# Attention and a token/channel mixer on one core: v of a head in one transfer, a weight group in two, and a new order of all work

## The chip, the cores and the metric

The kernel runs on one core of a Trainium2 chip. The number that counts is the time of one execution on the device, in microseconds. The kernel before was run three times: median 972.38 us, from 970.54 to 972.43. One further execution was profiled; it took 971.08 us, and the span from its first to its last instruction is 969.3 us.

Engines are named as the profile names them: PE is the matrix engine, PEld its weight loads, DVE the vector engine, ACT the scalar engine, POOL the GpSimd engine. SP issues the transfers; in the profile its own queue is SPq.

## The reference

Eight batches, eight heads, 576 positions, 64 numbers per head. Everything is float32.

```python
scores = scale * np.matmul(q, k.transpose(0, 1, 3, 2))
cum = np.cumsum(np.log(np.clip(f, 0.0001, 1.0)), axis=-1)
decay = cum[:, :, :, None] - cum[:, :, None, :]
scores = np.where(causal, -1000000000.0, scores + decay)
attn = np.exp(scores - np.max(scores, axis=-1, keepdims=True))
attn = attn / (np.sum(attn, axis=-1, keepdims=True) + 1e-09)
out = np.matmul(attn, v)                       # 8 x 8 x 576 x 64
# the heads side by side are x: 8 x 576 x 512
h = np.maximum(x.transpose(0, 2, 1) @ w_tok1, 0.0) @ w_tok2    # over the positions, 256 wide
u = x + h.transpose(0, 2, 1)
result = u + np.maximum(u @ w_ch1, 0.0) @ w_ch2                # over the channels, 1536 wide
```

The weights arrive as 64-bit numbers and are turned into 32-bit ones on the chip.

## The kernel before

The program has two stages. In the first (0 to about 434 us of the span) the 64 heads are worked off as 32 pairs, two heads of a batch at a time, one on each half of the 128 partitions. Per pair, q and k come in one transfer (line 716, buffer raw, three of them). v comes in four transfers, two per head (line 720, buffer vr, two of them): five blocks of 64 positions to one place, four blocks to another. The decay comes as a broadcast row (line 728, buffer cb, two of them). PE makes the scores (lines 743 and 749), DVE adds the decay and takes the smallest negated score (line 784), ACT takes the exponential and its sums (line 788). PE turns the probabilities (line 862), ACT or DVE copies them out of PSUM into pf (lines 872 and 870), and PE multiplies them with v (lines 891 and 894). The sums are inverted on DVE, turned on PE (line 834), stored to memory in rows of 3 KB (line 840, recd<-rs) and loaded back as broadcast rows (line 845, rb). POOL multiplies them into the result, xt (line 920). After every second pair half a batch is mixed over the positions: PE turns it (line 1244), and two products follow (line 1227, weights t1 and t2, the value held as a high and a low part in xn and ring). The sum goes to memory (line 1313, ud).

Beside this, 24 groups of channel weights are decoded in the first stage: each comes in four transfers of 128 x 128 numbers (line 557, d_raw<-in_w_ch), passes ACT, DVE and POOL, and is stored in two transfers (line 638, wd<-sg).

In the second stage PE does the channel products, 2520 matmuls over 128 x 128 weights (lines 1045 to 1047 and 1110 to 1112), with weights loaded back by line 960. A few of them stand already in the first stage.

The order is fixed by hand, as it were: the table ORDER names for every engine the sequence of its operations, and each engine works its list strictly in that sequence, waiting where something is not there yet. For SP this means that a transfer whose buffer is not free yet holds up all transfers behind it. A planner (class Plan) replays the lists with assumed durations; from this come only the assignment of buffers to slots and the order of the code. All transfers but two are issued by SP and run on one queue.

Of the kernel before, what the change touches and what calls it, by code (L numbers as in the profile page):

```python
# [9 lines left out]
F32 = mybir.dt.float32  # L10
# [5 lines left out]
P = 128  # L16

PRM = dict(
    FILL=36, ND=1, n_raw=3, n_vr=2, n_cb=2, n_rb=2, n_pr=2, n_pf=4, n_xn=1,
# [47 lines left out]
    ),  # L67
    DVE=(
# [205 lines left out]
class Plan:  # L274
# [48 lines left out]
    def run(self, slots):  # L323
# [45 lines left out]
        while left:  # L369
            more = True  # L370
            while more:
                more = False
                for e, q in queue.items():
# [28 lines left out]
                    if e == "SP":  # L402
                        dma_at = max(end + 650, dma_at) + o.lat
                        done = dma_at + 980
# [34 lines left out]
def build(nc, env, dims):  # L439
# [39 lines left out]
    def at(b):  # L479
        return env[b.kind][b.slot]  # L480
# [1035 lines left out]
```

## Time and profile before

| | |
|---|---|
| median of three runs | 972.38 us (970.54 to 972.43) |
| the profiled execution, its span | 971.08 us, 969.3 us |
| mean granted clock of PE over the span | 0.986 |
| PE busy | 932.6 us, 96% |
| DVE busy | 722.2 us, 75% |
| ACT busy | 528.9 us, 55% |
| POOL busy | 237.2 us, 24% |
| mean rate of all transfers | 251 GB/s |
| the chain that ended last | PE 72%, DMA 13%, DVE 8%, ACT 2%, SPq 2% |

How to read it: the table averages over two stages with different limits. ACT and POOL have most of their work in the first stage alone, so their low shares say little. The chain is the sequence of work that ended last, followed back from the end; a share of it by DMA is time in which the last thing still missing was a transfer under way.

### The profile page before, as it was taken

How to read it: one execution, taken by the hardware profiler on the slowest of the kernel's cores; microseconds unless marked ns; L12 is line 12 of the kernel's file. 1: busy time of each engine (PE TensorE's matmuls, PEld its weight loads, DVE VectorE, ACT ScalarE, POOL GpSimd, SP SyncE). 2: the span in 40 equal slices, each digit the busy share in tenths (PEclk: the TensorE clock that was granted, in tenths of full speed). 3: DMA queues.
4: the chain of work that ended last, by engine and by line, in shares of the span. 5: the costliest groups of instructions: out<-in, count | busy, mean ns of one | idle time of the engine just before them, and what ended most of it. 6: DMA issues, size and time to landing. Idle time of an engine off the chain costs nothing.

```text
span 969.3 us, 27342 instructions
## 1 busy us (share of the span) xinstructions
PE 932.6 (96%) x10368; PEld 807.1 (83%) x10368; DVE 722.2 (75%) x1930; ACT 528.9 (55%) x1372; POOL 237.2 (24%) x320
## 2 busy tenths in 40 slices
PE   8899999999999999999999999999999999999998
PEld 5677777777778888888888888888888899989997
DVE  6998887878778876745599638973699538964586
ACT  5877888978878887842255114521254215521242
POOL 3567767765665641110000000000000000000000
PEclk9899999999999999999999999999999999999999
DMA  7889989898899978457877797888878787877874
GB/s 225 248 241 287 292 249 280 246 303 247 249 292 271 283 233 275 146 174 236 292 240 254 247 283 250 250 274 288 260 234 250 246 270 241 247 230 259 285 224 144
DMA packets 152211, 243.43 MB, mean 251 GB/s; under 512 B 22096, under 2 KB 82768, under 8 KB 152080
## 3 DMA queue, kind: packets, MB, share of 16 engines
q1 hardware_dynamic: 151984, 241.54, 80.6%
q8 instruction: 82, 1.34, 0.6%
q14 instruction: 49, 0.40, 0.1%
q10 hardware_dynamic: 96, 0.15, 0.0%
HBM read 200.38 MB, written 41.24 MB: 249 GB/s over the span
## 4 chain that ended last, share of the span: by engine, by line
PE 72%; DMA 13%; DVE 8%; ACT 2%; SPq 2%; issue 2%; POOL 1%; POOLq 0%; DVEq 0%; ACTq 0%
PE bank L1110 9%; PE bank L1112 9%; PE bank L1111 9%; PE bank L1045 9%; PE bank L1047 9%; PE bank L1046 9%; PE bank L1227 6%; PE bank L743 5%; DVE pr L784 3%; PE bank L891 3%; DMA cb<-decd 3%; DMA vr<-in_v 2%; PE bank L862 2%; DMA rb<-recd 2%; DMA raw<-in_qk 1%
## 5 line engine op out<-in xcount | busy, mean ns | idle before, releaser
L788 ACT ACTIVATE pr<-pr,nmin 128x448 f32<-128x448 f32 (+4 forms) x320 | 177.0, 558 | 27.7 <-DVE nmin L784 27.1
L487 ACT ACTIVATE st<-H 128x464 fp32r<-128x464 f32 (+1 forms) x210 | 119.9, 587 | 122.3 <-PE bank L1111 68.0
L1110 PE MATMUL bank<-st,wq 128*128 128x464 f32 (+1 forms) x420 | 156.0, 371 | 0.0
L1111 PE MATMUL bank<-st,wq 128*128 128x464 f32 (+1 forms) x420 | 155.9, 371 | 0.0
L1112 PE MATMUL bank<-st,wq 128*128 128x464 f32 (+1 forms) x420 | 155.8, 371 | 0.1
L784 DVE CUSTOM_DVE_ANT_0 pr<-bank,cb 128x448 f32<-128x448 f32 (+3 forms) x310 | 129.5, 452 | 24.4 <-DMA cb<-decd 9.7
L743 PE MATMUL bank<-raw 64*64 64x448 f32 (+6 forms) x1408 | 120.1, 408 | 9.6 <-DVE nmin L784 5.0
L496 DVE TENSOR_TENSOR st<-H,st 128x464 fp32r<-128x464 f32 (+1 forms) x150 | 91.7, 630 | 19.4 <-ACT st L487 15.9
L891 PE MATMUL bank<-pf,vr 64*64 64x128 f32 (+3 forms) x2048 | 98.8, 320 | 4.5 <-DMA vr<-in_v 3.0
L981 DVE TENSOR_TENSOR tmp<-bank,tmp 128x464 f32<-128x464 f32 (+1 forms) x80 | 50.1, 631 | 58.1 <-PE bank L1047 52.3
L872 ACT ACTIVATE pf<-bank 128x512 f32<-128x512 f32 x152 | 85.0, 594 | 12.4 <-PE bank L862 7.3
L891 PEld LDWEIGHTS bank<-pf,vr 64*64 64x64 f32 x2048 | 76.1, 136 | 17.3 <-ACT pf L872 4.2
L1112 PEld LDWEIGHTS bank<-st,wq 128*128 128x128 f32 x420 | 78.8, 188 | 9.7 <-DVE st L496 0.5
L743 PEld LDWEIGHTS bank<-raw 64*64 64x64 f32 x1408 | 57.0, 137 | 35.6 <-issue 12.5
L1110 PEld LDWEIGHTS bank<-st,wq 128*128 128x128 f32 x420 | 78.8, 188 | 9.2 <-DVE tmp L981 0.2
L1111 PEld LDWEIGHTS bank<-st,wq 128*128 128x128 f32 x420 | 78.8, 188 | 8.9
L862 PE MATMUL bank<-ident,pr 64*128 64x64 f32 x1536 | 68.9, 230 | 6.3 <-DVE nmin L784 4.0
L1057 ACT ACTIVATE tmp<-bank 128x464 f32<-128x464 f32 (+1 forms) x30 | 16.6, 554 | 105.7 <-PE bank L1047 105.6
L862 PEld LDWEIGHTS bank<-ident,pr 64*128 64x128 f32 x1536 | 62.4, 143 | 11.8 <-DVE nmin L784 3.8
L920 POOL TENSOR_TENSOR xt<-xt,rb 128x512 f32<-128x512 f32 (+1 forms) x64 | 51.4, 819 | 79.9 <-DMA rb<-recd 36.6
L1227 PE MATMUL bank<-t2h,ring 64*128 64x288 f32 x512 | 62.8, 308 | 0.3 <-DVE nmin L784 0.2
L788 ACT ACTIVATION_READ_ACCUMULATOR pr<-pr,nmin 128x1 f32 (+1 forms) x320 | 62.4, 195 | 0.0
(172 smaller groups left out, 2099.7 us busy)
## 6 DMA issues: line engine op xcount, KB each, us to landing
wq<-wd SPq DMA_DIRECT2D x420, 256.0 KB
raw<-in_qk SPq DMA_DIRECT2D x32, 576.0 KB
cb<-decd SPq DMA_DIRECT2D x31, 576.0 KB
d_raw<-in_w_ch SPq DMA_DIRECT2D x96, 128.0 KB
wd<-sg SPq DMA_DIRECT2D x24, 512.0 KB
rb<-recd SPq DMA_DIRECT2D x64, 144.0 KB
wd<-sg SPq DMA_DIRECT2D x24, 384.0 KB
ud<-xt SPq DMA_DIRECT2D x16, 576.0 KB
```

The lines of the kernel that those rows point to most:

```text
L487: nc.scalar.activation(out, in_, func, scale=scale)
L496: nc.vector.tensor_tensor(out, in_, asf(hi), op=ALU.subtract)
L743: nc.tensor.matmul(at(buf)[HALF[h], of : of + n], q[:, i0 : i0 + D], k[:, j0 : j0 + n], start=t not in (0, 1), stop=not nd, skip_group_che ...
L784: nc.vector.tensor_tensor_reduce(o, x, y, -1.0 / D**0.5, c0[:m, NS + z : NS + z + 1] if t == 5 else 3e38, op0=ALU.add, op1=ALU.min, accum_ ...
L788: nc.scalar.activation(x, x, AF.Exp, bias=E["nmin"][sm][:m, t : t + 1], scale=-1.0, accum_out=E["sums"][sm // 2][:m, sm % 2 * (NS + 1) + ( ...
L862: nc.tensor.transpose(at(ps[s])[:, k * D : (k + 1) * D], at(pr)[r, x, :, :].rearrange("p a b -> p (a b)"), E["ident"][r, r])
L891: nc.tensor.matmul(at(av[z])[o, 256 - w : 256], at(vr)[r, vblk(j), :], at(pt)[r, c : c + w], start=j == 4, stop=gi == 2, skip_group_check= ...
L1045: nc.tensor.matmul(o, wt[:, 0, :], h_, start=(first and k == 0), stop=False, skip_group_check=True)
L1110: nc.tensor.matmul(o, wt[:, 0, :], h_, start=(first and x == 0), stop=False, skip_group_check=True)
L1111: nc.tensor.matmul(o, wt[:, 1, :], h_, start=False, stop=False, skip_group_check=True)
L1112: nc.tensor.matmul(o, wt[:, 0, :], l_, start=False, stop=(x == FX - 1), skip_group_check=True)
L1227: last[s] = nc.tensor.matmul(at(ps[s ^ z])[:, : width[0]], a, m, start=(z == 0 and i == 0), stop=(z == 1 and i == len(todo[s]) - 1), skip_ ...
```

## The change

v of a head comes in one transfer that fills ten blocks (one block is loaded twice, so that both halves have the same length), and a weight group comes in two transfers. The buffer vr becomes one block longer. The planner assumes 1950 ns in place of 980 ns from the data to the signal of a transfer, and the special rates of two kinds of transfer are dropped. The table ORDER is another one for all five engines. What is computed is the same; on PE both programs hold the same number of matmuls of every line. All line numbers of the first stage move down by four to six.

```diff
-    FILL=36, ND=1, n_raw=3, n_vr=2, n_cb=2, n_rb=2, n_pr=2, n_pf=4, n_xn=1,
+    FILL=36, ND=(0,), n_raw=3, n_vr=2, n_cb=2, n_rb=2, n_pr=2, n_pf=4, n_xn=1,
...
 ORDER = dict(
     PE=(
-        "14:27 147 41:4 148 137 157:2 138 45 141 46 199 142 216 202 47:3 207 175 178 181 169 184:3 282 290 285 233 236 "
+        "14:29 145 139 135:2 140 155 146 156 43:4 195 47:3 203 198 212 173 176 167 179 182:3 276 279 284 293 229 223 "
...
                     if e == "SP":
                         dma_at = max(end + 650, dma_at) + o.lat
-                        done = dma_at + 980
+                        done = dma_at + 1950
...
         def ld(rows, cols, src):
-            o = at(rb)[rows, cols, :]
+            o = at(rb)[rows, cols, :] if hi else at(rb).rearrange("p (a b) two -> p a b two", b=P)[:, cols]
             nc.sync.dma_start(o, src.bitcast(U32).rearrange("... (n two) -> ... n two", two=2))
...
         for x, (b, z0, z1) in enumerate(((pb, 0, 3), (sb, 3, 7))):
             dma(
-                lambda b=b, z0=z0, z1=z1: nc.sync.dma_start(E["w_d"][which][q][:, z0:z1, k], asf(at(b)[:, : z1 - z0])), P * 1024 * (z1 - z0), rate=340,
+                lambda b=b, z0=z0, z1=z1: nc.sync.dma_start(E["w_d"][which][q][:, z0:z1, k], asf(at(b)[:, : z1 - z0])), P * 1024 * (z1 - z0),
...
-            def src(row, half):
+            def src(half):
                 if which == 1:
-                    return w_ch1[sl((k + 2 * half) * P, P), sl((a + row) * P, P)]
-                return w_ch2[sl((a + half) * P, P), sl((2 * row + k) * P, P)]
-
-            loads = [(full, sl(n * P, P), src(row, half)) for n, (row, half) in enumerate(((0, 0), (0, 1), (1, 1), (1, 0)))]
+                    return w_ch1[sl((k + 2 * half) * P, P), sl(a * P, 2 * P)].rearrange("p (r c) -> p r c", c=P)
+                return w_ch2[sl((a + half) * P, P), :].rearrange("p (r k c) -> p r k c", k=2, c=P)[:, :, k, :]
+
+            loads = [(full, cols, half) for half, cols in enumerate((slice(0, 4, 3), slice(1, 3)))]
+            loads = [(full, cols, src(half)) for _, cols, half in loads]
             return lambda: unit(loads, which, q, k, i)
...
         for s in (0, 1):
-            for x, (r, a, z) in enumerate(((HALF[0], 0, NS), (HALF[1], NS, 2 * NS - 1))):
-                dma(
-                    lambda vr=vr, n2=n2, s=s, r=r, a=a, z=z: nc.sync.dma_start(at(vr)[HALF[s], a:z, :], E["v"][n2][r, s * NS + NS - (z - a) : s * NS + NS, :]),
-                    D * (z - a) * D * 4, dur=515, rate=220, wr=[(vr, s, x)], bufs=[vr],
-                )
-        v_in = [(vr, s, x) for s in (0, 1) for x in (0, 1)]
+            dma(
+                lambda vr=vr, n2=n2, s=s: nc.sync.dma_start(
+                    at(vr)[HALF[s]].rearrange("p (x n) e -> p x n e", x=2), E["v"][n2].rearrange("(x d) n e -> d x n e", x=2)[:, :, s * NS : (s + 1) * NS, :]
+                ),
+                D * 2 * NS * D * 4, dur=515, wr=[(vr, s)], bufs=[vr],
+            )
+        v_in = [(vr, s) for s in (0, 1)]
...
-        ("vr", [P, 2 * NS - 1, D], F32),
+        ("vr", [P, 2 * NS, D], F32),
```

On SP, the transfers from the first to the last piece of v of the fourth pair (vr_194 is one of the two v buffers, d_raw the weights still to be decoded, rs the turned inverse sums) stood like this before:

```order
L720 DMA vr_194<-in_v 64x256
L557 DMA d_raw_161<-in_w_ch 128x256
L720 DMA vr_194<-in_v 64x320
L557 DMA d_raw_161<-in_w_ch 128x256
L840 DMA recd<-rs_102 12x64
L557 DMA d_raw_161<-in_w_ch 128x256 x2
L840 DMA recd<-rs_102 12x64
L716 DMA raw_190<-in_qk 128x1152
L720 DMA vr_194<-in_v 64x320
L720 DMA vr_194<-in_v 64x256
```

After the change the same stretch of SP, again from the first to the last piece of v of the fourth pair, reads:

```order
L714 DMA vr_194<-in_v 64x2x320
L551 DMA d_raw_162<-in_w_ch 128x2x256
L836 DMA recd<-rs_102 12x64 x2
L551 DMA d_raw_161<-in_w_ch 128x512
L714 DMA vr_194<-in_v 64x2x320
```

Four pieces of v over eleven transfers have become two over six. Counted for all 32 pairs in the two lists, the last piece stood on average 12.2 transfers behind the first, and stands 5.7 behind it now.

On PE, the turning of the inverse sums of the ninth pair (line 834, from rec) stood in the midst of a mixing product (line 1227, ring is the hidden value, t2 the weight) before:

```order
L1227 MATMUL bank_69<-t2l,ring_157 128x288
L1227 MATMUL bank_68<-t2h,ring_158 128x288
L1227 MATMUL bank_69<-t2h,ring_158 128x288
L834 MATMUL bank_63<-ident,rec_96 64x64 x2
L1227 MATMUL bank_69<-t2h,ring_157 128x288
L1227 MATMUL bank_68<-t2h,ring_157 128x288
L1227 MATMUL bank_69<-t2l,ring_157 128x288
L1227 MATMUL bank_68<-t2l,ring_157 128x288
```

In the changed list the same turning of the ninth pair (now line 830) has the product with v ahead of it (line 887) and scores behind it (line 739):

```order
L887 MATMUL bank_63<-pf_203,vr_193 64x256 x2
L887 MATMUL bank_65<-pf_203,vr_193 64x256 x2
L887 MATMUL bank_63<-pf_203,vr_193 64x256 x2
L887 MATMUL bank_65<-pf_203,vr_193 64x256 x2
L830 MATMUL bank_67<-ident,rec_96 64x64 x2
L739 MATMUL bank_68<-raw_191 64x320
L739 MATMUL bank_69<-raw_191 64x320
L739 MATMUL bank_68<-raw_191 64x256
```

The scores, the product with v and the turning of the sums use PE in quarters of 64 x 64, the turning of the probabilities and the mixing in halves of 64 x 128, the channel products as a whole. Up to the last mixing matmul the list changed between these forms 128 times before, and changes 108 times now.

## Rows read from the trace of the kernel before

**Rows 1.** Busy time by stretch: length, each engine's busy us, PE clock, DMA share, GB/s.

```profile
0.00:120.00 120.00, 107.44 (x1874) 84.54 (x1878) 102.19 (x371) 90.26 (x269) 73.95 (x107) 0.93 0.85 260
120.00:360.00 240.00, 225.68 (x4632) 190.07 (x4628) 194.39 (x720) 201.32 (x610) 150.54 (x198) 0.98 0.88 265
360.00:440.00 80.00, 75.87 (x1385) 65.55 (x1375) 53.04 (x177) 54.37 (x157) 12.68 (x17) 1.00 0.63 200
440.00:970.00 530.00, 523.59 (x2493) 466.91 (x2493) 372.59 (x665) 183.00 (x339) 0.00 (x0) 1.00 0.80 251
```

**Rows 2.** Waits of PE, whole span: who waited for whom, us, times, longest.

```profile
PE bank L743 <- DVE nmin L784: 5.0, 7, 1.7
PE bank L862 <- DVE nmin L784: 4.0, 4, 1.5
PE bank L1244 <- POOL xt L920: 3.3, 3, 1.5
PE bank L891 <- DMA vr<-in_v: 3.0, 3, 1.3
...
PE bank L743 <- DMA raw<-in_qk: 2.0, 1, 2.0
```

**Rows 3.** Groups by line: busy us, mean ns, then idle time ahead and its releasers.

```profile
L784 DVE CUSTOM_DVE_ANT_0 pr<-bank,cb 128x448 f32<-128x448 f32 (+3 forms) x310 | 129.5, 452 | 24.4 <-DMA cb<-decd 9.7 <-PE bank L743 5.9 <-PE bank L749 5.8
...
L920 POOL TENSOR_TENSOR xt<-xt,rb 128x512 f32<-128x512 f32 (+1 forms) x64 | 51.4, 819 | 79.9 <-DMA rb<-recd 36.6 <-PE bank L1227 18.7 <-ACT xt L915 13.7
```

**Rows 4.** Chain that ended last, its transfers: start us, us, what.

```profile
127.62 4.13 DMA vr<-in_v
...
149.12 6.78 DMA cb<-decd
...
347.92 5.34 DMA recd<-rs
```

**Rows 5.** SP's queue in order of time: start us, us, the issue.

```profile
124.03 0.45 SPq L845 DMA_DIRECT2D rb<-recd  x1
124.53 0.59 SPq L720 DMA_DIRECT2D vr<-in_v  x1
125.17 1.05 SPq L557 DMA_DIRECT2D d_raw<-in_w_ch  x2
126.27 0.71 SPq L845 DMA_DIRECT2D rb<-recd  x1
127.08 0.50 SPq L840 DMA_DIRECT2D recd<-rs  x1
127.62 0.48 SPq L720 DMA_DIRECT2D vr<-in_v  x1
```

**Rows 6.** Issues of two lines: count, shortest, median and longest ns, first and last.

```profile
L720 SPq DMA_DIRECT2D vr<-in_v x128: 465/492/1541, 17.2 to 410.8; - x128
...
L557 SPq DMA_DIRECT2D d_raw<-in_w_ch x96: 327/469/1742, 38.4 to 321.1; - x96
```

**Rows 7.** Page, transfers by queue: packets, MB, share of 16 engines' span.

```profile
q1 hardware_dynamic: 151984, 241.54, 80.6%
```

**Rows 8.** PE in order of time where the ninth pair's sums are turned.

```profile
124.28 0.30 PE L1227 MATMUL bank<-t2l,ring 64*128 64x288 f32 x2
124.41 0.30 PE L1227 MATMUL bank<-t2h,ring 64*128 64x288 f32 x2
124.72 0.33 PE L834 MATMUL bank<-ident,rec 64*64 64x64 f32 x4
124.98 0.40 PE L1227 MATMUL bank<-t2h,ring 64*128 64x288 f32 x2
```

**Rows 9.** Busy time in two short stretches, columns as in group 1.

```profile
20.00:22.00 2.00, 0.48 (x15) 0.23 (x6) 1.64 (x7) 1.15 (x4) 0.00 (x0) 1.00 1.02 366
...
24.00:26.00 2.00, 2.00 (x36) 1.74 (x32) 2.00 (x9) 1.65 (x7) 1.28 (x3) 0.50 0.89 333
```

More of the change, by code (lines that the diff above doesn't have):

```diff
@@ L696, in vblk @@
     def vblk(j):
-        return 0 if not j else (j + 1) // 2 if j % 2 else 4 + j // 2
+        return 0 if not j else (j + 1) // 2 if j % 2 else NS + j // 2
     def streams(g):
@@ L713, in build @@
         p.batch = b
-        nd = n2 < ND
+        nd = n2 in ND
         raw, vr, pr = Buf("raw"), Buf("vr"), Buf("pr")
```

414 rows, old and new, of tables (ACT, DVE, PE, POOL) are left out of this document.

## The prediction

> **What bounds the kernel now.** I read the busy time by stretch first, since the page's 96% for PE is an average over two stages. From 440 us to the end PE is busy 523.59 us of the 529.3 us that are left of the span, at full clock [rows 1]. Of the missing 5.7 us most is the end, after the last matmul. There PE is the bound, its matmuls are the same ones before and after, and no order of transfers can shorten them. So the change has only the first 440 us to work on.
>
> In these 440 us PE is idle 12.6 us up to 120, 14.3 us from 120 to 360 and 4.1 us from 360 to 440, 31.0 us together [rows 1]. The granted clock is 0.93 in the first of these stretches and 0.98 in the second: 0.07 x 120 + 0.02 x 240 = 13.2 us worth of full-speed time that was not granted. What can be won at all is therefore some 44 us, if work per matmul stays as it is. But no other engine is slack either: from 120 to 360 DVE is at 81%, ACT at 84%, the transfers at 0.88. A stage in which everything is this full loses its time in many small waits.
>
> The waits of PE come next [rows 2]. The two largest are for DVE's minima (5.0 and 4.0 us), then POOL's scaled result (3.3), v (3.0, three times) and q and k (2.0, once). DVE and POOL are late themselves, and the groups by line say why [rows 3]: of the 24.4 us that DVE idles ahead of the minima, 9.7 end with the decay row (cb); of the 79.9 us that POOL idles ahead of the scaling, 36.6 end with the inverse sums (rb). Passing these shares on, 9.7/24.4 of 9.0 us is 3.6, and 36.6/79.9 of 3.3 us is 1.5. With v and q, k, transfers that land late cost PE 3.0 + 2.0 + 3.6 + 1.5 = 10.1 us. That is the part that this change can reach directly.
>
> Why are they late? The chain shows legs of 4.13 us (v), 6.78 us (cb) and 5.34 us for a transfer of only 3 KB (recd) from issue to landing [rows 4]. Ahead of such an issue, SP itself is the queue: from 124.03 to 128.10 it spends 0.45 + 0.59 + 1.05 + 0.71 + 0.50 + 0.48 = 3.78 of 4.07 us issuing, and the v transfer of 127.62, on which PE then waits, is the last of these [rows 5].
>
> **The change, part by part.** Fewer issues. v drops from 128 to 64, the weight groups from 96 to 48. At the medians of 492 and 469 ns [rows 6] that is 31.5 + 22.5 = 54.0 us of SP's time within some 400 us. The merged issue describes twice as many pieces, and no row shows one. If it takes twice as long, the saving is zero; if it takes the same, 54 us. I take nearly the same, since weight pieces over 128 partitions (469 ns) are issued no slower than v pieces over 64 (492 ns).
>
> What that is worth at PE: the last piece of v stood 12.2 transfers behind the first and now stands 5.7 behind. At SP's pace in the stretch shown, 4.07 us for seven issues or 0.58 us each, v is complete 3.8 us earlier after its buffer comes free. The largest single wait on v is 1.3 us, so I take the whole 3.0 us away. The other 7.1 us (cb, rb, q and k) are not merged; they only move up in a shorter queue. Bounds: 0 and 7.1. I take a quarter, 1.8, because their legs of 5 to 7 us lie mostly behind the issue. Next late, where v is no longer, is DVE: a wait of PE for the minima is the likeliest to fill the place.
>
> Form changes of PE. The list changes form 128 times up to the last mixing matmul before and 108 times now. At the ninth pair, two mixing matmuls start 0.13 us after the two ahead of them (124.28 to 124.41), but with the turning in between 0.57 us pass (124.41 to 124.98) [rows 8]. The extra 0.44 us holds two changes and the turning itself, so one change costs at most 0.22 us, and at least nothing. I take 0.15, and 20 fewer give 3.0 us (0 to 4.4).
>
> More bytes. A head's v loads ten blocks in place of nine: 64 x 16 KB = 1.05 MB more, at 265 GB/s [rows 1] 4.0 us of all transfer engines. They are idle 12% of the stretch. If that idle time takes it, the cost is zero; if not, 4.0 us. I take half, 2.0. The weight bytes are unchanged.
>
> Clock. In the first stage the clock falls to its lower level behind gaps: PE is busy 0.48 of 2 us at 20 to 22, and from 24 to 26 the clock is 0.50, 1.2 in place of 2.4 GHz [rows 9]. If 4.8 us of 31.0 us of gaps go, I let the same 15% of the 13.2 us go, 2.0 us. Bounds: 0, and 6 if half of the low stretches go.
>
> The new order otherwise. Where a block moves past another it trades one wait for another; the trace of before cannot show the new ones. Bounds by the nearest rows: all of DVE's 9.0 us [rows 2] won, or as much lost once more. I take zero. Six channel matmuls more stand ahead of the last mixing matmul; they are only moved from the second stage, at the same price. The second stage, POOL's decode steps and the end are costed at nothing: same instructions, and PE's 99% there covers the rest. Were that cover gone, the weight loads on the one queue would be late first.
>
> Sum: 3.0 + 1.8 + 3.0 + 2.0 - 2.0 = 7.8 us less than the profiled execution's 971.08 us, or 963.3. That execution lies 1.3 us below the median of the runs, inside their spread, so I forecast 963.
>
> **Rivals.** The first, slower: the transfer engines, not SP, are what the legs wait for. For it speaks the 3 KB transfer that takes 5.34 us [rows 4]: size cannot be its price, so it stands behind other bytes, and one queue holds nearly all of them, 241.54 MB [rows 7]. The Trainium skill, DMA: Bandwidth & Descriptors, section on queues, rings and completion order, says that each transfer engine consumes the descriptors of one issuing queue in ring order; the trace's small slow transfer agrees. The place is 120 to 360, where the share is already 0.88 and SP would now feed the engines sooner without their draining faster. It decides once the share there comes to about 0.95. Then the 4.0 us of bytes are paid in full, and the 10.1 us of late transfers grow by half, 5 us, with 2 us of clock behind the gaps; the 3.0 us of form changes are still won. That gives 971.1 + 11 - 3 = 979. Against it: the share averages 0.88, and v's bytes grow by a ninth only.
>
> The second, a larger gain: SP is the bound of 40 to 360. Then all 10.1 us go, half of the clock loss (6 us) and the form changes (3.0): 971.1 - 19 = 952. For it speaks SP's 93% in the stretch shown; against it, that legs of 5 to 7 us lie behind the issue. The Trainium skill, same page, section on the anatomy of one DMA, fits a fixed part of about 2.0 us and bytes at 436 GB/s to a transfer that GpSimd issues; by that estimate v of a pair would fall from 8.7 to 4.8 us, 125 us over 32 pairs, if transfers went singly. The trace disagrees with singly: 265 GB/s are moved with many under way at once.
>
> The third, no change: merged issues take twice as long, v's pieces still meet full engines, and the new order wins and loses in equal parts. Form changes and bytes nearly cancel: 971 to 973. For it: transfers account for a third of PE's idle time, and DVE and ACT above 80% will make other waits in their place. That the change does not do what it says is unlikely: both lists show 64 and 48 transfers fewer.
>
> **How the numbers follow.** Forecast (955 to 969): 0.52. Larger gain (945 to 955): 0.15. No change: 0.12. Slower (974 to 985): 0.21. A measurement here tells about 0.2% from no change, 1.9 us around the median of 972.38. The forecast's upper edge adds a little to no change and the rest is read off: faster 0.67, same 0.12, slower 0.21. With a tenth left out at each end the range is 950 to 979.
>
> **What would show it.** Right: PE's wait for v below 0.5 us; SP's issues of v at about 0.5 us each; PE idle below 26 us in the first 440 us with the mean clock above 0.986; the last mixing matmul some 8 us earlier and the second stage as long as before. Wrong, towards slower: a DMA share above 0.92 from 120 to 360 and longer legs in the chain. Wrong, towards no change: the same idle time with DVE's minima as the releaser throughout. My sum fails altogether if the second stage changes its length by more than 2 us.

## The result and the profile after

The changed kernel takes 947.12 us (median of 4 runs, 945.93 to 948.45) against 972.4 us before: ratio 0.9727, 95% interval 0.9677 to 0.9777. I had forecast 963 with a range of 950 to 979. Faster was right; the size, 9 us of 25, was not.

The profiled execution took 945.93 us, its span is 944.2 us. Busy time by stretch, to be held against [rows 1]:

```profile
0.00:120.00 120.00, 106.25 (x2036) 84.00 (x2038) 104.59 (x398) 96.39 (x288) 71.72 (x107) 0.99 0.90 263
120.00:360.00 240.00, 231.01 (x4870) 199.27 (x4864) 202.31 (x753) 211.07 (x642) 156.50 (x206) 1.00 0.94 286
360.00:440.00 80.00, 78.03 (x1093) 68.07 (x1091) 49.88 (x137) 42.80 (x118) 6.51 (x8) 0.98 0.64 207
440.00:970.00 530.00, 499.75 (x2388) 447.92 (x2387) 363.24 (x644) 178.08 (x328) 0.00 (x0) 1.00 0.77 241
```

From 120 to 360 us, PE finishes 4870 matmuls in place of 4632. Its idle time in the first 440 us is 13.75 + 8.99 + 1.97 = 24.7 us in place of 31.0, and the clock that was not granted is worth 0.01 x 120 + 0.02 x 80 = 2.8 us in place of 13.2. Both are smaller. DVE, ACT and the transfers are all busier than before in the middle stretch: the whole stage runs faster, not one engine.

Where the first stage ends can be read from PE in order of time:

```profile
412.43 0.29 PE L1223 MATMUL bank<-t2l,ring 64*128 64x288 f32 x2
412.56 0.29 PE L1223 MATMUL bank<-t2h,ring 64*128 64x288 f32 x2
412.78 0.48 PE L1041 MATMUL bank<-ring,wq 128*128 128x464 f32 x1
```

Before, the last of them was:

```profile
437.49 0.29 PE L1227 MATMUL bank<-t2h,ring 64*128 64x288 f32 x2
```

The last mixing matmul ends at 412.85 us; before, it ended at 437.78. That is 24.9 us. From there to the end it is 531.35 us now and was 531.5 before. So the gain lies in the first stage alone. Most of it is not idle time of PE. PE's busy time, for the same 10368 matmuls, was 932.6 us before and is now:

```profile
PE 915.0 (97%) x10368; PEld 799.3 (85%) x10368; DVE 720.0 (76%) x1930; ACT 528.3 (56%) x1372; POOL 234.7 (25%) x320
```

Of the 24.9 us, 6.3 are idle time of PE, 10.4 are clock, if each stretch of low clock is counted in full, and some 8 are left, in the main busy time of PE that is shorter for another reason.

The waits of PE [rows 2]:

```profile
PE bank L830 <- DVE rec L822: 4.5, 10, 0.8
PE bank L739 <- DVE nmin L780: 2.5, 4, 0.9
...
PE bank L887 <- DMA vr<-in_v: 1.6, 3, 1.0
```

The two waits for DVE's minima were 9.0 us together; POOL's result (3.3 us) is gone from the list, v fell from 3.0 to 1.6 us. One wait grew, that for the inverse sums (L830): 4.5 us where it was 1.5. The groups by line [rows 3]:

```profile
L780 DVE CUSTOM_DVE_ANT_0 pr<-bank,cb 128x448 f32<-128x448 f32 (+3 forms) x310 | 129.2, 452 | 10.6 <-PE bank L745 4.5
...
L916 POOL TENSOR_TENSOR xt<-xt,rb 128x512 f32<-128x512 f32 (+1 forms) x64 | 50.9, 812 | 57.3 <-DVE nmin L780 22.3
```

DVE idled 24.4 us ahead of the minima, for cb more than for anything else (9.7); now it is 10.6, and PE is the first releaser. POOL idled 79.9 us, for rb more than for anything else (36.6); now 57.3, with DVE first. Transfers no longer stand first in either row. Yet the transfers themselves are no quicker, as far as the chain shows them. Its legs, from issue to landing [rows 4]:

```profile
217.90 3.16 DMA vr<-in_v
...
263.25 5.14 DMA vr<-in_v
321.08 7.62 DMA cb<-decd
```

They last 3 to 8 us, as before. What changed is when they are issued. SP's queue in order of time [rows 5]:

```profile
121.28 1.80 SPq L841 DMA_DIRECT2D rb<-recd  x1
124.50 0.73 SPq L836 DMA_DIRECT2D recd<-rs  x2
125.32 0.34 SPq L724 DMA_DIRECT2D cb<-decd  x1
125.77 1.81 SPq L632 DMA_DIRECT2D wd<-sg  x2
127.89 0.57 SPq L551 DMA_DIRECT2D d_raw<-in_w_ch  x1
128.91 0.39 SPq L632 DMA_DIRECT2D wd<-sg  x1
```

From 121.28 to 129.30 SP issues for 5.64 of 8.02 us, where it did for 3.78 of 4.07 before. Both stretches are short, and that of before is a crowded one. Added up over the timeline from 40 to 360 us, SP issued for 236.8 us (74%) before and issues for 203.0 us (63%) now; its waits in these 320 us add up to 94.9 us before and 122.4 us now. (A wait can end within the issue that it holds up, so the two overlap in part.) In the list of SP's own waits over the whole span two have grown most:

```profile
SPq L836 <- ACT rs L833: 35.2, 18, 7.0
...
SPq L841 <- DMA recd<-rs: 20.0, 15, 2.8
```

Before, they were:

```profile
SPq L845 <- DMA recd<-rs: 12.6, 8, 3.4
...
SPq L840 <- ACT rs L837: 5.7, 5, 2.2
```

SP now waits longer for the data that it is to transfer: it comes to these places earlier than the work does. The issues of the two merged lines [rows 6]:

```profile
L714 SPq DMA_DIRECT2D vr<-in_v x64: 600/632/1702, 15.6 to 380.6; - x64
L551 SPq DMA_DIRECT2D d_raw<-in_w_ch x48: 339/580/1566, 37.8 to 319.7; - x48
```

A merged issue takes 632 and 580 ns at the median, 28% and 24% longer than a piece did. At medians, v and weights cost SP 64 x 0.632 + 48 x 0.580 = 68.3 us in place of 63.0 + 45.0 = 108.0: 39.7 us saved, not 54.0. The queue's totals [rows 7]:

```profile
q1 hardware_dynamic: 148656, 242.58, 83.2%
```

1.04 MB more, as worked out, with 2% fewer packets.

### The profile page after: what moved, and what is told of

Read it like the earlier page. It is cut to its first block, busy times and chain, and to the rows that moved or that the text cites. A ratio compares the mean times of both kernels' runs of the same rounds, so it can differ in the third digit from the quotient of the medians.

```text
span 944.2 us, 27174 instructions
## 1 busy us (share of the span) xinstructions
PE 915.0 (97%) x10368; PEld 799.3 (85%) x10368; DVE 720.0 (76%) x1930; ACT 528.3 (56%) x1372; POOL 234.7 (25%) x320
## 4 chain that ended last, share of the span: by engine, by line
PE 85%; DVE 7%; DMA 4%; ACT 2%; issue 2%; POOL 0%; SPq 0%; DVEq 0%; ACTq 0%; POOLq 0%
PE bank L1223 11%; PE bank L1043 9%; PE bank L1041 9%; PE bank L1042 9%; PE bank L1106 9%; PE bank L1107 9%; PE bank L1108 9%; PE bank L739 6%; PE bank L887 6%; PE bank L858 4%; DVE pr L780 3%; DMA vr<-in_v 2%; PE bank L1240 1%; DMA cb<-decd 1%; ACT pf L868 1%
## 5 line engine op out<-in xcount | busy, mean ns | idle before, releaser
L784 ACT ACTIVATE pr<-pr,nmin 128x576 f32<-128x576 f32 (+4 forms) x320 | 176.8, 557 | 15.7 <-DVE nmin L780 15.0
L780 DVE CUSTOM_DVE_ANT_0 pr<-bank,cb 128x448 f32<-128x448 f32 (+3 forms) x310 | 129.2, 452 | 10.6 <-PE bank L745 4.5
L739 PE MATMUL bank<-raw 64*64 64x448 f32 (+6 forms) x1408 | 111.9, 395 | 5.5 <-DVE nmin L780 2.5
L868 ACT ACTIVATE pf<-bank 128x512 f32<-128x512 f32 x152 | 84.0, 594 | 10.1 <-PE bank L858 6.3
L1106 PEld LDWEIGHTS bank<-st,wq 128*128 128x128 f32 x420 | 78.9, 188 | 10.1 <-DVE xt L1145 1.1
L739 PEld LDWEIGHTS bank<-raw 64*64 64x64 f32 x1408 | 55.1, 133 | 25.2 <-issue 10.8
L858 PE MATMUL bank<-ident,pr 64*128 64x64 f32 x1536 | 65.4, 225 | 4.8 <-issue 1.7
L858 PEld LDWEIGHTS bank<-ident,pr 64*128 64x128 f32 x1536 | 59.6, 139 | 8.9 <-issue 2.5
L1059 ACT ACTIVATE H<-bank 128x464 f32<-128x464 f32 (+1 forms) x30 | 16.4, 552 | 88.2 <-PE bank L1043 88.2
L916 POOL TENSOR_TENSOR xt<-xt,rb 128x512 f32<-128x512 f32 (+1 forms) x64 | 50.9, 812 | 57.3 <-DVE nmin L780 22.3
```

The source lines that it names most:

```text
L739: nc.tensor.matmul(at(buf)[HALF[h], of : of + n], q[:, i0 : i0 + D], k[:, j0 : j0 + n], start=t not in (0, 1), stop=not nd, skip_group_che ...
L780: nc.vector.tensor_tensor_reduce(o, x, y, -1.0 / D**0.5, c0[:m, NS + z : NS + z + 1] if t == 5 else 3e38, op0=ALU.add, op1=ALU.min, accum_ ...
L784: nc.scalar.activation(x, x, AF.Exp, bias=E["nmin"][sm][:m, t : t + 1], scale=-1.0, accum_out=E["sums"][sm // 2][:m, sm % 2 * (NS + 1) + ( ...
L858: nc.tensor.transpose(at(ps[s])[:, k * D : (k + 1) * D], at(pr)[r, x, :, :].rearrange("p a b -> p (a b)"), E["ident"][r, r])
L868: p.op("ACT", d_act(512), lambda src_=src_, o=o: nc.scalar.activation(o(), src_(), AF.Copy), rd=[ps[s]], wr=[(pt, s)], bufs=[ps[s], pt])
L1106: nc.tensor.matmul(o, wt[:, 0, :], h_, start=(first and x == 0), stop=False, skip_group_check=True)
```

## Experiments

Theory S: the first stage was bound by SP, by the time that it needs to issue its list of transfers. Rival T: the transfer engines, by the number, packets or bytes of the transfers that they work off. Rival O: the new order. Rival C: the clock. All times below are medians against the kernel before in the same job (972.35 to 974.0 us), with the ratio's 95% interval; the last two columns are how long SP issues between 40 and 360 us (before: 236.8, the changed kernel: 203.0) and how long it waits for rs in the whole span (before: 5.7, the changed kernel: 35.2). The second is a rough sign of SP's slack only: tiny_transfers, as slow as the kernel before, has 15.2.

| run | us | ratio | interval | SP issues, us of 320 | SP waits for rs, us |
|---|---|---|---|---|---|
| order_alone | 966.75 | 0.9936 | 0.9902 to 0.9970 | 239.7 | 14.8 |
| merge_alone | 957.31 | 0.9831 | 0.9778 to 0.9885 | 195.1 | 18.3 |
| order_w_merged | 952.50 | 0.9785 | 0.9729 to 0.9841 | 227.4 | 21.1 |
| order_v_merged | 945.40 | 0.9705 | 0.9654 to 0.9756 | 226.1 | 27.8 |
| tiny_transfers | 972.11 | 1.0010 | 0.9982 to 1.0039 | 237.8 | 15.2 |
| tiny_v_only | 954.19 | 0.9818 | 0.9756 to 0.9879 | 221.5 | 18.0 |
| more_bytes | 960.55 | 0.9853 | 0.9787 to 0.9918 | 219.3 | 17.6 |
| clock_fill | 974.69 | 1.0019 | 0.9985 to 1.0053 | 234.5 | 3.8 |
| after_again | 945.69 | 0.9707 | 0.9666 to 0.9747 | 197.0 | 40.0 |
| order_v_again | 949.12 | 0.9726 | 0.9682 to 0.9770 | 221.4 | 29.3 |
| tiny_pool | 956.99 | 0.9821 | 0.9768 to 0.9875 | 190.2 | 44.6 |
| tiny_act | 998.04 | 1.0234 | 1.0186 to 1.0282 | 159.2 | 48.3 |
| order_pool | 948.83 | 0.9758 | 0.9680 to 0.9837 | 214.4 | 39.0 |
| before_pool | 958.66 | 0.9852 | 0.9781 to 0.9924 | 211.4 | 19.9 |

**Taking the change apart.** order_alone keeps the new order and splits v and the weights again, the pieces standing where the merged transfer stood; order_w_merged splits v alone, order_v_merged the weights alone. merge_alone keeps the old order and puts the merged transfer where its first piece stood. The edit for v in order_alone, on the changed kernel:

```diff
-            dma(
-                lambda vr=vr, n2=n2, s=s: nc.sync.dma_start(
...
+            for x in (0, 1):
+                a, z = x * NS + 1 * x, (x + 1) * NS
+                dma(
+                    lambda vr=vr, n2=n2, s=s, x=x, a=a, z=z: nc.sync.dma_start(at(vr)[HALF[s], a:z, :], E["v"][n2][HALF[x], s * NS + NS - (z - a) : s * NS + NS, :]),
```

> The new order with the old transfers: each transfer of v stands as two again (five and four blocks), each of a weight group as two again, at the place of the merged one in the new list. Theory 1, the order with the clock that it keeps up makes the gain: 949 to 955 us, low-clock time under 10 us. Theory 2, fewer issues on SP make it: 962 to 972 us, with PE's waits for v back at 3 us or more. Theory 3, neither does without the other: about half, 957 to 962.

> The old order with the new transfers: a merged transfer stands where the first of its two pieces stood. Theory 1 (order): 966 to 973 us. Theory 2 (fewer issues): 949 to 957 us, idle time of PE in the first 440 us below 25. Theory 3: 958 to 965.

> The new order, weight groups in two transfers, v of a pair in four again. Theory 1: within 3 us of the changed kernel, 946 to 950. Theory 2: v is what counts since PE waits on it, so 955 us or more. Under both the 64 issues of v at 0.49 us come back on SP.

> The new order, v of a head in one transfer, weight groups in four again. Theory 1: within 3 us of the changed kernel, 946 to 950. Theory 2: the 48 issues of weights at 0.47 us come back: 23 us of SP time, and 951 to 957 us.

The order alone brings 5.6 us, the merging alone 15.1, both 25.3 or so. The order is worth more once the transfers are merged (957.3 to 947.1, 10 us) than while they are split. On the new order, merging the weights brings 14.3 us and merging v 21.4, but both together no more than v alone: the gain saturates. The middle stretch of merge_alone and of order_alone:

```profile
120.00:360.00 240.00, 229.26 (x4752) 193.48 (x4746) 199.37 (x739) 207.97 (x625) 153.56 (x201) 1.00 0.95 280
```

```profile
120.00:360.00 240.00, 223.87 (x4635) 191.52 (x4634) 199.39 (x722) 201.90 (x613) 151.70 (x200) 0.99 0.88 270
```

With the old order on every engine, merging alone takes the transfers' share to 0.95, the very point from which I had let the engines decide for slower, and the kernel is 15 us faster. So O is a part of the gain, 5.6 to 10 of 25.3 us, and not the whole, and fewer bytes are not what the merging gives: it moves 1.04 MB more.

**Giving the issues back.** tiny_transfers is the changed kernel with one transfer of 512 bytes, into memory that nobody reads, on SP ahead of each merged transfer; tiny_v_only has only the 64 ahead of v. more_bytes has the 64 with 64 KB each, 4.2 MB in all.

```diff
+    def tiny():
+        nc.sync.dma_start(E["tiny_d"].pop(), E["mask"][:16, :8])
+
...
-                lambda vr=vr, n2=n2, s=s: nc.sync.dma_start(
+                lambda vr=vr, n2=n2, s=s: tiny() or nc.sync.dma_start(
```

> The changed kernel, with one additional transfer of 512 bytes on SP ahead of each merged transfer of v (64) and of weights (48): SP issues as often as before the change, the transfer engines get practically no bytes more. Theory A, SP's issue time is what the merging freed: 958 to 967 us, as the new order with the old transfers (966.75). Theory B, the transfer engines or the later landing of the second piece are what the merging freed: 946 to 950 us.

> As the run before, but only the 64 small transfers ahead of v. Theory A: 949 to 956 us (the new order with only the weights merged took 952.5). Theory B: 946 to 949 us.

> The changed kernel, with one additional transfer of 64 KB on SP ahead of each merged transfer of v: 64 issues and 4.2 MB more, 16 us of all transfer engines at 265 GB/s. Against the run with 64 small ones only the bytes differ. Theory A: the bytes cost less than half of this, under 8 us, since the engines drain what SP gives them. Theory C, the transfer engines are the bound at a share of 0.94: 12 to 20 us more than with the small ones.

112 issues with 57 KB between them cost the whole gain. The middle stretch of tiny_transfers, its 112 issues, and SP's queue:

```profile
120.00:360.00 240.00, 214.51 (x4419) 183.34 (x4418) 190.57 (x686) 192.62 (x583) 144.43 (x186) 0.98 0.85 262
```

```profile
L477 SPq DMA_DIRECT2D tiny<-mask x112: 303/528/1977, 15.0 to 412.6; - x112
```

```profile
123.68 0.54 SPq L716 DMA_DIRECT2D raw<-in_qk  x1
124.27 0.48 SPq L846 DMA_DIRECT2D rb<-recd  x1
124.80 0.58 SPq L637 DMA_DIRECT2D wd<-sg  x1
125.43 0.50 SPq L716 DMA_DIRECT2D raw<-in_qk  x1
125.98 1.02 SPq L477 DMA_DIRECT2D tiny<-mask  x1
127.04 1.12 SPq L719 DMA_DIRECT2D vr<-in_v  x1
128.21 0.66 SPq L477 DMA_DIRECT2D tiny<-mask  x1
128.96 0.40 SPq L556 DMA_DIRECT2D d_raw<-in_w_ch  x1
```

SP issues for 5.30 of 5.68 us again, and from 40 to 360 us for 237.8 us, as before the change. The transfer engines' share falls to 0.85: they are given less to do. PE's waits show where that lands:

```profile
PE bank L1245 <- POOL xt L921: 7.7, 7, 1.8
PE bank L892 <- DMA vr<-in_v: 5.6, 4, 2.3
PE bank L744 <- DMA raw<-in_qk: 5.1, 2, 4.4
```

The first 64 issues cost 7 us, the next 48 cost 18. This fits slack that is used up first: of the runs above, order_v_merged with its 48 issues more lost nothing against the changed kernel, order_w_merged with 64 lost 5 us, order_alone with both 20. The packets are not it: the small transfers add 3584 to the queue, those of more_bytes add 9216, and more_bytes is 11.6 us faster. Nor do bytes weigh much: 4.16 MB more than tiny_v_only are 15.7 us of engine time at 265 GB/s and cost 6.4 us, with intervals that overlap.

**The clock by itself.** clock_fill is the kernel before with 228 idle transposes put on PE ahead of turnings (lines 862 and 1244) at seven places, to keep its clock up.

```diff
+WARM_T = {0: 60, 7: 20, 21: 24, 50: 44}
+WARM_X = {2: 44, 11: 12, 16: 24}
...
+    def warm(ps, n):
+        for k in range(n):
+            r = slice(D * (k % 2), D * (k % 2) + D)
+            nc.tensor.transpose(at(ps[k % 2])[:, :D], E["mask"][r, :P], E["ident"][r, r])
```

> The kernel before, with idle transposes written to the bank that the following operation fills anyway, at seven places where PE idled 0.6 to 2.2 us and the clock fell afterwards (60, 20, 24 and 44 ahead of turnings of probabilities, 44, 12 and 24 ahead of turnings for the mixing). Theory D, the low stretches are a cost by themselves: with some four of the seven gone 963 to 968 us. Theory E, the clock costs little since other engines set the pace in these stretches: 970 to 975 us.

Its first 440 us:

```profile
0.00:120.00 120.00, 108.04 (x2074) 87.15 (x2078) 101.40 (x378) 91.55 (x274) 75.59 (x107) 0.97 0.84 260
120.00:360.00 240.00, 220.78 (x4566) 184.43 (x4558) 189.32 (x702) 197.27 (x595) 149.20 (x196) 1.00 0.87 262
360.00:440.00 80.00, 75.02 (x1432) 66.04 (x1430) 52.90 (x183) 56.25 (x166) 13.63 (x17) 0.98 0.64 194
```

The clock not granted falls from 13.2 to 3.6 + 0 + 1.6 = 5.2 us, and PE's idle time rises from 31.0 to 12.0 + 19.2 + 5.0 = 36.2; the time stays. This does not decide between D and E. The 228 transposes alone keep PE busy for 9.32 us, the first figure behind the length in this row:

```profile
0.00:440.00 440.00, 9.32 (x228) 8.10 (x228) 0.99 0.82 249
```

That is about as much as the 8.0 us of clock that came back, and at all seven places the turning starts without a gap behind the last transpose, so they may have held it up. What the clock is worth by itself is not shown. As a cause beside the transfers C is answered by other runs: merge_alone keeps PE's list, and 5.2 us of clock are not granted in place of 13.2; tiny_transfers only adds small transfers to the changed kernel, and 2.8 us become 8.8. The clock follows the transfers and is one of the ways in which their lateness reaches PE.

**Who issues.** The small transfers of tiny_transfers still leave two readings: SP's time, or the number of transfers. In tiny_pool and tiny_act GpSimd and ScalarE issue the same 112. after_again and order_v_again are the measure beside them.

```diff
-        nc.sync.dma_start(E["tiny_d"].pop(), E["mask"][:16, :8])
+        nc.gpsimd.dma_start(E["tiny_d"].pop(), E["mask"][:16, :8])
```

> As tiny_transfers (112 transfers of 512 bytes, one ahead of each merged transfer of v and of the weights), but GpSimd issues them, not SP. If the loss of tiny_transfers (25 us) is SP's time of issuing, most of it is gone: 947 to 955 us, the rest being what GpSimd pays for its own issues. If it is the number of transfers that the engines work off, whoever issues them, the loss stays: 965 to 976 us.

> The same 112 transfers, issued by ScalarE. ScalarE was at 84% from 120 to 360 us, so its own issues cost something too. SP's time as the cause: below 960 us, and SP's waits for others as long as in the changed kernel. The number of transfers as the cause: 965 to 976 us.

> The changed kernel once more, as the measure for the other three of this job: 946 to 949 us.

> New order, v merged, weights in four transfers, once more beside the changed kernel (945.4 us against 947.1 in two different jobs). If SP's queue has stopped being the bound once v is merged, the 48 issues more cost nothing: within 2 us of the changed kernel. If each issue still cost what the 48 weight issues cost in tiny_transfers against tiny_v_only ((972.1 - 954.2) / 48 = 0.37 us), it would be 18 us slower than the changed kernel.

From GpSimd the same transfers cost 11 us, not 25. SP is free again (44.6 us of waits for rs), and GpSimd pays with its own time:

```profile
L477 POOL DMA_DIRECT2D tiny<-mask x112: 487/547/903, 15.5 to 392.3; - x112
```

112 x 0.547 = 61 us. The time of tiny_act met neither expectation: 52 us slower than the changed kernel, worse than from SP. The issues themselves, 112 x 0.309 = 34.6 us, do not make 52. Its profiled execution was the slowest of its six, 1012.42 us against 995.21 to 999.40, so the lines show who waits for whom and not what the 52 us are made of. PE waits for ACT, and ACT for transfers of which it uses nothing:

```profile
PE bank L835 <- DVE rec L827: 9.6, 9, 3.6
PE bank L863 <- ACT pf L873: 9.0, 7, 5.8
```

```profile
ACT pr L789 <- DMA vr<-in_v: 10.6, 3, 5.9
...
ACT pr L789 <- DMA tiny<-mask: 7.4, 2, 6.2
```

The changed kernel has no such waits of ACT. In the traces SP's transfers report their landing by eight semaphores in turn, and nearly every one (1028 of 1091 before) waits until the last one on its semaphore, the eighth ahead of it, has landed. ScalarE's 112 transfers here use the same eight, so ACT waits for SP's transfers; GpSimd's use eight others. tiny_act therefore does not price an issue on ScalarE, and its 48.3 us of SP's waits for rs, which ACT makes, are no sign of slack. What counts is tiny_pool: the same 112 transfers cost less than half as much from GpSimd as from SP, which a price per transfer at the engines could not do. order_v_again and after_again differ by 3.4 us with intervals that overlap: 48 weight issues more are not told from nothing, 18 us are excluded.

The last pair changes the issuer, and with it the queue and the moment of the issue; number and size of the transfers are those of their base. order_pool is order_alone, before_pool the kernel before, with the second piece of v of each head issued by GpSimd, 64 of 128.

```diff
-                    lambda vr=vr, n2=n2, s=s, r=r, a=a, z=z: nc.sync.dma_start(at(vr)[HALF[s], a:z, :], E["v"][n2][r, s * NS + NS - (z - a) : s * NS + NS, :]),
+                    lambda vr=vr, n2=n2, s=s, r=r, a=a, z=z, x=x: (nc.gpsimd if x else nc.sync).dma_start(at(vr)[HALF[s], a:z, :], E["v"][n2][r, s * NS + NS - (z - a) : s * NS + NS, :]),
```

> As order_alone (new order, v in 128 and the weights in 96 transfers; 966.75 us), but GpSimd issues the second piece of each v, 64 transfers. Number and size of the transfers are the same. If SP's time of issuing is the bound, SP is relieved as by merging v (order_v_merged: 945.4 us), less some 6 us for GpSimd's own 64 issues (half of tiny_pool's 11): 948 to 958 us. If the number of transfers is the bound, nothing is relieved and GpSimd pays: 967 to 975 us.

> The kernel before with the same edit: GpSimd issues 64 of the 128 v transfers. SP's time as the bound: merge_alone won 15.1 us with 112 issues fewer; 64 of them are 8.6 us, less up to 6 us that GpSimd pays in its own order: 963 to 970 us. The number of transfers as the bound: 973 to 980 us.

order_pool is 18 us faster than order_alone, and their intervals don't meet; before_pool is 15 us faster than before, more than S had expected. Two rows of order_pool, the middle stretch and the issues:

```profile
120.00:360.00 240.00, 229.28 (x4829) 196.31 (x4824) 208.38 (x745) 208.89 (x633) 177.49 (x246) 1.00 0.91 282
```

```profile
L724 SPq DMA_DIRECT2D vr<-in_v x64: 465/477/1385, 15.1 to 381.9; - x64
L724 POOL DMA_DIRECT2D vr<-in_v x64: 516/577/910, 16.2 to 381.8; - x64
```

The same number and size of transfers, 64 of them issued elsewhere, and nearly the whole gain of the change is there. That rules out T as a price per transfer at the engines, whoever issues them. What these runs don't tell apart is SP's own time from a limit of the one queue on which it issues, since GpSimd's transfers run on another:

```profile
q0 software_dynamic: 2048, 4.20, 1.7%
```

Fewer issues relieve both, and the small transfers on SP load both. One limit stands in the program: with eight semaphores, at most eight of SP's transfers are under way. Waits for the landing of transfers whose data the next one does not use are in SP's list of before:

```profile
SPq L557 <- DMA raw<-in_qk: 6.0, 6, 1.8
SPq L720 <- DMA cb<-decd: 6.0, 5, 2.0
```

All waits of SP for landings other than recd's come to 42.5 us between 40 and 360 us before. merge_alone has 40.1 us of them, issues for 195.1 us in place of 236.8 and is 15 us faster, which speaks for the time of issuing. No run gave SP's transfers more semaphores, so the limit of eight stays open. The Trainium skill, DMA: Bandwidth & Descriptors, section on issuing engines not being separate DMA queues, says that issuing from several engines saves only the sequencer's time of issuing, which is usually small beside the transfer. Whether it is only that time is not shown here; what issuing from a second engine saved, 18 us, was not small.

No run beat the changed kernel by more than its interval.

## Why the prediction was wrong, point by point

**The step that failed** is the one on the late transfers that are not merged: "The other 7.1 us (cb, rb, q and k) are not merged; they only move up in a shorter queue. ... I take a quarter, 1.8, because their legs of 5 to 7 us lie mostly behind the issue." Two things are wrong in it. The legs start at the issue; what a transfer waited for its turn in SP's queue is not in them. The legs are as long after as before, and the stage is 25 us shorter. And the reach of the change was read off PE's waits, 10.1 us. With PE's list unchanged, merge_alone won 15.1 us: lateness of the queue also came to PE as DVE, ACT and POOL that were late in their turn, and as clock. The sum of the waits on the engine at the end is no cap for what a queue that feeds all engines can give back.

In the terms of the sum, PE's idle time is the small part of the miss: 4.8 us were to go and 6.3 went. The larger part is what hung on it: "If 4.8 us of 31.0 us of gaps go, I let the same 15% of the 13.2 us go". 20% of the gaps went and with them 79% of the clock that was not granted, 10.4 us in place of 2.0. In the trace of merge_alone, where PE's list is the old one, idle time is 4.0 us less and the clock not granted 8.0.

**The rival that held** is the second, SP as the bound of 40 to 360, to which I gave 0.15. What spoke for it pointed the right way, SP's 93% in the stretch shown [rows 5], though from 40 to 360 us it was 74%; what I held against it, the long legs, was no evidence at all. Its 952 was too modest for the same reason as the sum. That SP waited only 5.7 us for rs in the trace of before, of 94.9 us of waits from 40 to 360, does not decide it: rs waits of 14.8 and 15.2 us stand beside times of 966.75 and 972.11. What decides is that issues added to SP, and taken from it, moved the time (tiny_transfers, before_pool, order_pool); whether by SP's time or by a limit of its queue stays open. The Trainium skill, Perfetto Trace Analysis, section on what DMA-bound means, names the issuing engine's sequencer, solid with issues, as a bound of its own beside the transfer engines. [rows 5] agree for their 4 us; over the stage SP's track was 74% issues and not solid.

**The first rival** took a DMA share above 0.92 as the sign of slower. The share came to 0.94 and the kernel was faster: with more of the stage's transfers in the same 240 us (286 GB/s in place of 265) the share must rise, and it is no sign of slower. The small transfer of 5.34 us [rows 4] may show that transfers stand behind others; it did not show that this was the limit.

**Fewer issues.** I took a merged issue as nearly as long as a piece; it is 24 to 28% longer, and 39.7 us were saved in place of 54.0. This miss is in the other direction and small beside the rest.

**v.** Waits of 3.0 us fell to 1.6, not below 0.5.

**Form changes and order.** 3.0 us for 20 form changes and zero for the order otherwise. order_alone holds both and wins 5.6 us, some 10 on top of merging. In its trace PE's busy time is 11.0 us shorter than before, 6.4 of them clock, and its idle time 7.1 us longer; some 4.6 us are left for form changes and anything else, near the 3.0 forecast. The form changes were not measured apart.

**Bytes.** 2.0 us, half of 4.0. more_bytes cost 6.4 of 15.7 us, which fits half, though not beyond its uncertainty.

**Clock.** 2.0 of 13.2 us were to come back, 6 at most; 10.4 did. It came back with the transfers (merge_alone) and went with them (tiny_transfers); clock_fill does not show what it is worth alone.

**The second stage** kept its length, within 0.2 us, as forecast.

## What to carry to other kernels

Look at the queue that issues as at any other engine: how much of a crowded stretch it spends issuing, over the whole stage and not only in its fullest microseconds, and what it waits for. PE's waits did not show that SP's queue held this stage back; adding small issues to it, and giving some of its issues to another engine, did. The remedies were fewer issues, or another issuer that has slack and a queue of its own. A leg from issue to landing tells nothing of the time a transfer waited for its issue.

## What was not expected of the hardware

The same 512-byte transfer took 309 ns to issue from ScalarE, 528 from SP and 547 from GpSimd (medians of 112). From SP the shortest was 303 ns, so about two fifths of SP's median is time beyond the shortest issue; what it is was not tried and stays open. On the same engine, v's pieces took 594 ns in order_alone and 477 in order_pool, where half as many were left to it.
